# Keeping a weight fold's eight small products together on TensorE

## The chip, the cores and the metric

The kernel runs on one core of a Trainium2 chip. The metric is the device time of one launch in microseconds (us). The times of the kernel before are those of three runs; the trace comes from one more, profiled execution.

## What is computed

Nyström attention over 4 batches and 8 heads, followed by two feed-forward layers over all 2304 tokens, everything in float32 with double inputs for the weights:

```python
def _attn_ref(q, k, v):                      # (4, 8, 576, 64)
    q_lm, k_lm = ...                         # 32 landmarks: means over 18 rows
    A, Bm, C = sm(q, k_lm), sm(q_lm, k_lm), sm(q_lm, k)
    Z = Bm.T / (norm1 * norminf + 1e-06)
    for _ in range(6):
        Z = 2 * Z - Z @ Bm @ Z
    return A @ Z @ C @ v

x = attn_out.transpose(0, 2, 1, 3).reshape(B * S, H * D)
x = ((x @ w_a) * (x @ w_b)) @ w_out          # 512 -> 1536 -> 512
h = x @ w_in                                 # 512 -> 2048
g = h * np.tanh(softplus(h))
out = g @ w_out2                             # 2048 -> 512
```

## The kernel before

The attention output is never formed. For a batch b the small matrix M = Z C v (32 by 64 for each head) is multiplied into the first layer's weights: this is the **fold**. `MT[b]` holds M, two heads' halves on 64 partitions each; `wab[g]` holds columns of `w_a` and `w_b`, 256 of each, for group g (six groups of 512 columns). For one (b, g) the fold is eight products: 64 rows of `MT[b]` by 32 columns as the stationary operand, 64 rows by 512 columns of `wab[g]` as the moving one, each into its own 32 partitions of one of two PSUM banks (`ps_bm`, one pair buffer). ScalarE then copies the pair to `bm` (high part), and VectorE writes the remainder (low part). There are 4 x 6 = 24 folds. A product of float32 is two LDWEIGHTS and MATMUL records in the trace, so a fold has 16 records.

The layer itself follows in 96 slots, `ab(b, g, hf, ch)`: two halves of six 128x288 matmuls each (`ps_ab<-at,bm`), an evacuation by ScalarE (`ta`), a product by VectorE (`tg`), and a split of the result into `g1` by ScalarE and GpSimd. `emit_o1` sums `ps_o1<-g1,wo1`, six 128x288 matmuls for each half, and VectorE or ScalarE adds them to `x2acc`. The second layer (`ps_ab<-xc,wc` and the rest) begins at about 460 us and needs `x2acc` by way of DRAM (`x2d`, read as `xq`).

Weights arrive as float64 words in staging buffers (`stg`) through SyncE's DMA queue, and VectorE and ScalarE convert them (`wab`, `f`). A `wab` tile is filled in four pieces; columns j = 2 and 3 of its second axis come last. Each group is converted once, stored to DRAM and read back later through `load_wab`.

What sets the order on TensorE: the first part of the program is a list written by hand (`ORDER_1`), in which every instruction keeps the order of the text (`Written.on`). Four folds stand in it. After it `Written.on` is off, the slots are emitted in a loop, each calls `emit_bm` for the fold of a later slot, and a scheduler lays all instructions out by priority and by when it thinks that their inputs are there. A fold's eight products are independent for it, so it may put other matmuls between them. On each engine the chip then executes in the order that the scheduler wrote.

Of the kernel before, what the change touches and what calls it, by code (L numbers as in the profile page):

```python
# [31 lines left out]
def nystrom_moe_kernel(ctx: ExitStack, tc: tile.TileContext, q, k, v, w_a, w_b, w_out1, w_in2, w_out2, q1, k1, out):  # L32
# [30 lines left out]
    ac, pe, ve = Written(nc.scalar), Written(nc.tensor), Written(nc.vector)  # L63
# [18 lines left out]
    def pair_bank(tag):  # L82
        return two.get(tag, ps).tile([128, 2, 512], F32, tag=tag, bufs=1, name=f"ps_{tag}")
# [28 lines left out]
    MT = {}  # L112
# [382 lines left out]
    wab, converted = {}, {}  # L495
# [61 lines left out]

    def fold(b, g):
        p = pair_bank("bm")
        for c in range(2):  # L560
            r = slice(64 * c, 64 * c + 64)
            for j in range(4):
                pe.matmul(
                    p[32 * j:32 * j + 32, c], MT[b][r, 32 * j:32 * j + 32],
                    wab[g][r, j].rearrange("p a f -> p (a f)"), start=True, stop=True,
                )
        t = main.tile([128, 2, 2, 512], F32R, tag="bm", bufs=3, name="bm")
        yield
        ac.activation(t[:, 0], p, AF.Copy)
        yield  # L570
        ve.tensor_tensor(t[:, 1], p, t[:, 0].bitcast(F32), op=ALU.subtract)
        bm[b, g] = t

    def emit_bm(b, g):
        for _ in fold(b, g):
            pass
# [239 lines left out]
    for n in range(N_UNITS):  # L816
        part[f"c{n}"] = unit(n)
    part["f0"], part["f1"], part["F0"], part["F1"] = fold(0, 0), fold(0, 1), fold(1, 0), fold(1, 1)
    for n in range(N_SLOTS):
        b, m = divmod(n, 8)  # L820
        g, hf = (m // 2 % 2, m // 4) if b else (m // 4, m // 2 % 2)
# [97 lines left out]
    def product(k, n):  # L919
        p = bank("ab")  # L920
        w, x = wc[n], xs[n // 8, k]
        m = 0
        for j in range(2):
            for sl, sr in ((0, 0), (0, 1), (1, 0)):
                pe.matmul(p[:, 0:TB], w[:, sl, P_W[k], j], x[:, sr, j], start=(m == 0), stop=(m == 5))
                m += 1
        return p
# [39 lines left out]
    def early_product(k):  # L967
        Written.on = True
        p = product(k, 0)
        Written.on = False  # L970
        return p
# [10 lines left out]
    p = early_product(1)  # L982
# [5 lines left out]
    p = early_product(2)  # L988
# [89 lines left out]
    for n in range(24):  # L1078
# [7 lines left out]
        for gap, k in enumerate(ORDER):  # L1086
            if gap == 1 and n in (1, 2):
                last_stores.pop(0)[1]()
            if n == 0:
                p = None if k in ORDER[:3] else early_product(k)  # L1090
            else:
                p = product(k, n)
# [71 lines left out]
```

## Time and profile before

| | |
|---|---|
| median of three runs | 831.23 us (830.99 to 831.99) |
| the profiled execution's own time | 834.0 us |
| its span in the trace | 832.2 us |
| TensorE busy | 797.8 us, 96% of the span |
| VectorE, ScalarE, GpSimd busy | 541.7, 361.1 and 141.9 us |
| mean granted TensorE clock | 0.988 |

In the profile PE is TensorE's matmul side, PEld its weight loads, DVE VectorE, ACT ScalarE, POOL GpSimd, and SP SyncE. Nearly every instruction goes through one helper, so its line is L56; groups are told apart by tile: `ps_bm<-wab,mt` are the folds, `ps_o` stands for the banks of `emit_o1`. A row of the timeline gives start, duration, engine, line, operation, tiles, partitions by columns, and the number of instructions merged; in brackets is the idle time before it and what ended it. The ends of matmuls are modelled and overlap what follows, so the start of the next row is the better measure of what a row cost.

### The profile page before, as it was taken

How to read it: one execution, taken by the hardware profiler on the slowest of the kernel's cores; microseconds unless marked ns; L12 is line 12 of the kernel's file. 1: busy time of each engine (PE TensorE's matmuls, PEld its weight loads, DVE VectorE, ACT ScalarE, POOL GpSimd, SP SyncE). 2: the span in 40 equal slices, each digit the busy share in tenths (PEclk: the TensorE clock that was granted, in tenths of full speed). 3: DMA queues.
4: the chain of work that ended last, by engine and by line, in shares of the span. 5: the costliest groups of instructions: out<-in, count | busy, mean ns of one | idle time of the engine just before them, and what ended most of it. 6: DMA issues, size and time to landing. Idle time of an engine off the chain costs nothing.

```text
span 832.2 us, 14803 instructions
## 1 busy us (share of the span) xinstructions
PE 797.8 (96%) x5854; PEld 689.5 (83%) x5854; DVE 541.7 (65%) x1012; ACT 361.1 (43%) x824; POOL 141.9 (17%) x143
## 2 busy tenths in 40 slices
PE   5869999999999999999999999999999999999998
PEld 3356778997787887888889889988999999899997
DVE  7868887895498498886796765768433447433433
ACT  3645845444334344454353543554332335332332
POOL 1011212222141242222221344330000000000000
PEclk9889999999999999999999999999999999999999
DMA  9977466558527748868324887878645545555502
GB/s 353 293 280 257 149 233 219 194 179 285 184 68 250 290 143 300 283 209 292 108 93 133 324 335 276 303 280 344 215 179 237 217 185 232 215 192 224 191 0 76
DMA packets 48732, 183.44 MB, mean 220 GB/s; under 512 B 4260, under 2 KB 12452, under 8 KB 39320
## 3 DMA queue, kind: packets, MB, share of 16 engines
q1 hardware_dynamic: 39832, 169.40, 57.1%
q10 hardware_dynamic: 8832, 13.11, 4.3%
q8 instruction: 46, 0.75, 0.4%
q14 instruction: 22, 0.18, 0.1%
HBM read 129.02 MB, written 53.48 MB: 219 GB/s over the span
## 4 chain that ended last, share of the span: by engine, by line
PE 78%; DVE 8%; DMA 7%; ACT 3%; issue 3%; SPq 1%; ACTq 0%; POOL 0%; DVEq 0%
PE ps_ab L56 35%; PE ps_o L56 22%; PE ps_bm L56 12%; PE ps_at L56 10%; DMA tok<-in_k_dram 2%; DMA kt<-in_k_dram 2%; DVE f L56 2%; DMA vt<-in_v_dram 1%; DMA stg<-in_moe_w_a_dram 1%; DMA stg<-in_moe_w_out_dram 1%; ACT sa L56 1%; DVE wab L56 1%; DVE bm L56 1%; DVE tg L56 1%; DVE s L56 1%
## 5 line engine op out<-in xcount | busy, mean ns | idle before, releaser
L56 PE MATMUL ps_ab<-xc,wc 128*128 128x384 f32 x1008 | 197.1, 336 | 1.2 <-DVE u2s L56 1.0
L56 PE MATMUL ps_ab<-at,bm 128*128 128x288 f32 x1152 | 186.6, 302 | 4.7 <-DVE tg L56 3.5
L56 PEld LDWEIGHTS ps_ab<-xc,wc 128*128 128x128 f32 x1008 | 178.5, 188 | 12.5 <-DVE u2s L56 1.4
L56 PEld LDWEIGHTS ps_ab<-at,bm 128*128 128x128 f32 x1152 | 160.9, 189 | 30.2 <-issue 9.2
L56 PE MATMUL ps_o<-g,wo 128*128 128x288 f32 x1152 | 180.1, 299 | 3.7 <-ACT x2acc L56 3.0
L56 PEld LDWEIGHTS ps_o<-g,wo 128*128 128x128 f32 x1152 | 161.7, 190 | 18.4 <-issue 5.5
L608 POOL TENSOR_TENSOR g<-tg,g 128x288 fp32r<-128x288 f32 x96 | 88.7, 925 | 337.6 <-ACT g L56 274.2
L56 ACT ACTIVATE m<-c 128x384 f32<-128x384 f32 x95 | 49.6, 522 | 176.6 <-DVE c L56 174.5
L56 PE MATMUL ps_bm<-wo,g 128*128 128x512 f32 x288 | 92.8, 391 | 0.0
L56 DVE TENSOR_TENSOR g<-m,g 128x384 fp32r<-128x384 f32 x96 | 62.2, 650 | 30.5 <-ACT g L56 30.0
L56 PE MATMUL ps_at<-wo,g 128*128 128x512 f32 x288 | 81.5, 391 | 0.0
L56 PE MATMUL ps_o<-wo,g 128*128 128x512 f32 x288 | 78.7, 390 | 0.0
L56 DVE SCALAR_TENSOR_TENSOR f<-stg,f 128x512 uint32<-128x512 uint32 x88 | 69.8, 796 | 1.4
L56 ACT ACTIVATE g<-tg 128x288 fp32r<-128x288 f32 x96 | 42.4, 441 | 58.1 <-DVE tg L56 57.4
L56 ACT ACTIVATE ta<-ps_ab 128x288 f32<-128x288 f32 x96 | 38.9, 406 | 63.1 <-PE ps_ab L56 60.1
L56 PEld LDWEIGHTS ps_at<-wo,g 128*128 128x128 f32 x288 | 54.0, 188 | 10.2
L56 DVE TENSOR_TENSOR tg<-ps_ab,ta 128x288 f32<-128x288 f32 x96 | 43.3, 451 | 28.9 <-PE ps_ab L56 22.5
L56 PEld LDWEIGHTS ps_o<-wo,g 128*128 128x128 f32 x288 | 53.6, 188 | 8.7
L56 PEld LDWEIGHTS ps_bm<-wo,g 128*128 128x128 f32 x288 | 53.4, 188 | 6.3
L56 ACT ACTIVATE g<-m 128x384 fp32r<-128x384 f32 x96 | 50.4, 525 | 3.0
L56 DVE TENSOR_TENSOR u2s<-ps_ab,m 128x384 f32<-128x384 f32 x24 | 13.4, 557 | 57.9 <-PE ps_ab L56 57.9
L56 DVE TENSOR_TENSOR c<-ps_ab,m 128x384 f32<-128x384 f32 x23 | 12.8, 558 | 48.6 <-PE ps_ab L56 48.6
(156 smaller groups left out, 803.4 us busy)
## 6 DMA issues: line engine op xcount, KB each, us to landing
wc<-wcd SPq DMA_DIRECT2D x16, 1792.0 KB, 7.4
wo<-wod SPq DMA_DIRECT2D x16, 1024.0 KB, 9.5
stg<-in_moe_w_out_dram SPq DMA_DIRECT2D x28, 512.0 KB, 5.1
wcd<-wc SPq DMA_DIRECT2D x8, 1792.0 KB, 10.6
wab<-wabd SPq DMA_DIRECT2D x10, 1024.0 KB, 7.5
stg<-in_moe_w_in_dram SPq DMA_DIRECT2D x16, 512.0 KB, 6.0
wod<-wo SPq DMA_DIRECT2D x8, 1024.0 KB, 8.4
stg<-in_moe_w_a_dram SPq DMA_DIRECT2D x12, 512.0 KB, 7.4
```

What stands on the lines that cost most here:

```text
L56: i = f(*a, **kw)
L608: gp.tensor_tensor(t[:, 1], tg, t[:, 0].bitcast(F32), op=ALU.subtract)
```

## The change

The last piece of the weight tile is multiplied first, as an ordinary instruction; the other seven products are emitted at the scheduler's highest priority. So the one that must wait for the tile's last columns stands ahead, and behind it nothing else ready is preferred to the rest of the fold. The products, their operands and their number are the same.

```diff
     def fold(b, g):
         p = pair_bank("bm")
-        for c in range(2):
+        def piece(c, j):
             r = slice(64 * c, 64 * c + 64)
-            for j in range(4):
-                pe.matmul(
-                    p[32 * j:32 * j + 32, c], MT[b][r, 32 * j:32 * j + 32],
-                    wab[g][r, j].rearrange("p a f -> p (a f)"), start=True, stop=True,
-                )
+            pe.matmul(
+                p[32 * j:32 * j + 32, c], MT[b][r, 32 * j:32 * j + 32],
+                wab[g][r, j].rearrange("p a f -> p (a f)"), start=True, stop=True,
+            )
+
+        piece(0, 3)
+        with tc.high_priority():
+            for n in range(1, 8):
+                piece(n // 4, 3 - n % 4)
         t = main.tile([128, 2, 2, 512], F32R, tag="bm", bufs=3, name="bm")
```

What it does to the order: before, the 24 folds stand on TensorE in 39 places, 14 of them whole and 10 split in two to four; after it, in 24 places, all whole. Up to the first split fold the order on every engine is the same.

The first split fold, on TensorE, in the program's first third (x2 and x6 are the numbers of products, - is before, + is after):

```order
 L56 MATMUL ps_o_1298<-g_1191,wo_899 128x288 x3
-L56 MATMUL ps_bm<-wab,mt 32x512 x2
 L56 MATMUL ps_ab<-at,bm 128x288 x12
 L56 MATMUL ps_o_1349<-g_818,wo_620 128x288 x3
...
 L56 MATMUL ps_o_1349<-g_1191,wo_899 128x288 x3
-L56 MATMUL ps_bm<-wab,mt 32x512 x6
+L56 MATMUL ps_bm<-wab,mt 32x512 x8
 L56 MATMUL ps_ab<-at,bm 128x288 x6
```

The two products that stood ahead have joined the six; the matmuls between are where they were.

The first of the two folds that are split most, on TensorE, some 200 us into the program:

```order
 L56 MATMUL ps_o_2713<-g_2459,wo_2181 128x288 x3
 L56 MATMUL ps_o_2713<-g_2526,wo_2181 128x288 x3
-L56 MATMUL ps_bm<-wab,mt 32x512 x3
+L56 MATMUL ps_bm<-wab,mt 32x512 x8
 L56 MATMUL ps_at<-ident,E 128x128 x4
 L56 MATMUL ps_at<-ident,E 64x128
-L56 MATMUL ps_bm<-wab,mt 32x512
-L56 MATMUL ps_ab<-at,bm 128x288 x12
...
-L56 MATMUL ps_bm<-wab,mt 32x512
-L56 MATMUL ps_at<-rz 32x64 x8
-L56 MATMUL ps_ab<-at,bm 128x288 x12
-L56 MATMUL ps_bm<-wab,mt 32x512 x3
```

The fold's four places are now one, the first of them. From here on the scheduler lays out other matmuls anew too.

On SyncE's queue, where the second layer's first inputs (`xq`) are read among the loads of weights (`stg`), some 340 us into the program:

```order
 L416 DMA wab<-wabd_92 128x2048
 L441 DMA stg<-in_moe_w_in_dram 128x2x512
-L441 DMA stg<-in_moe_w_out_dram 128x1024
 L416 DMA xq<-x2d_83 128x2x384
 L416 DMA xq<-x2d_83 128x2x192
 L416 DMA xq<-x2d_84 128x2x192
-L441 DMA stg<-in_moe_w_out_dram 128x1024
+L441 DMA stg<-in_moe_w_in_dram 128x2x512
+L441 DMA stg<-in_moe_w_out_dram 128x1024 x2
```

The reads of `xq`, and the last reloads of `wab` with them, now stand ahead of two loads of weights that they stood behind, because the folds that free their buffers come earlier.

## Rows read from the trace of the kernel before

**Rows 1.** The page: busy time of each engine.
```profile
PE 797.8 (96%) x5854; PEld 689.5 (83%) x5854; DVE 541.7 (65%) x1012; ACT 361.1 (43%) x824; POOL 141.9 (17%) x143
```

**Rows 2.** Busy time by stretch of the span, all engines.
```profile
core 0: us, PE busy (x) PEld busy (x) DVE busy (x) ACT busy (x) POOL busy (x), PEclk, DMA share, GB/s
100.00:190.00 90.00, 87.64 (x738) 77.51 (x736) 75.46 (x145) 44.96 (x104) 21.23 (x24) 1.00 0.62 210
190.00:230.00 40.00, 40.00 (x403) 30.59 (x396) 20.18 (x47) 14.10 (x31) 7.96 (x9) 1.00 0.64 225
230.00:310.00 80.00, 78.96 (x871) 67.92 (x870) 62.03 (x132) 34.84 (x80) 23.65 (x26) 1.00 0.55 195
310.00:410.00 100.00, 99.14 (x733) 82.98 (x732) 78.65 (x137) 43.18 (x89) 25.09 (x26) 1.00 0.72 246
410.00:460.00 50.00, 47.66 (x334) 45.73 (x332) 39.82 (x70) 23.95 (x44) 11.19 (x12) 1.00 0.34 111
```

**Rows 3.** Whom TensorE waited for, 100 to 460: us, times, longest.
```profile
PE ps_ab L56 <- DVE tg L56: 3.1, 4, 1.0
PE ps_o L56 <- ACT x2acc L56: 1.2, 1, 1.2
PE ps_ab L56 <- ACT ta L56: 1.0, 2, 0.8
```

**Rows 4.** Timeline of TensorE around a split fold.
```profile
197.44 1.06 PE L56 MATMUL ps_bm<-wab,mt 64*32 64x512 f32 x6
198.43 0.76 PE L56 MATMUL ps_at<-ident,E 128*128 128x128 f32 x5
199.12 1.04 PE L56 MATMUL ps_bm<-wab,mt 64*32 64x512 f32 x2
200.10 1.86 PE L56 MATMUL ps_ab<-at,bm 128*128 128x288 f32 x12
201.79 1.75 PE L56 MATMUL ps_o<-g,wo 128*128 128x288 f32 x12
203.47 1.04 PE L56 MATMUL ps_bm<-wab,mt 64*32 64x512 f32 x2
204.45 0.43 PE L56 MATMUL ps_at<-rz 32*32 32x64 f32 x16
```

**Rows 5.** Timeline of TensorE where no small product is near.
```profile
141.66 1.76 PE L56 MATMUL ps_o<-g,wo 128*128 128x288 f32 x12
143.25 1.75 PE L56 MATMUL ps_ab<-at,bm 128*128 128x288 f32 x12
144.84 0.96 PE L56 MATMUL ps_o<-g,wo 128*128 128x288 f32 x6
```

**Rows 6.** Fold instructions alone: two stretches, then the whole group (busy, mean ns).
```profile
196.00:224.00 28.00, 7.36 (x32) 1.00 (x32) 0.00 (x0) 0.00 (x0) 1.00 0.61 208
263.00:274.00 11.00, 3.27 (x48) 0.54 (x48) 0.00 (x0) 0.00 (x0) 1.00 1.02 383
...
L56 PE MATMUL ps_bm<-wab,mt 64*32 64x512 f32 x384 | 42.0, 608 | 0.2 <-DVE bm L56 0.2
```

**Rows 7.** Chain that ended last, 95 to 131, and two rows of TensorE's timeline.
```profile
100.64 8.44 DMA stg<-in_moe_w_a_dram
117.20 8.28 DMA stg<-in_moe_w_out_dram
...
110.11 1.84 PE L56 MATMUL ps_o<-g,wo 128*128 128x288 f32 x12 [1.24 <-ACT x2acc L56]
129.17 1.86 PE L56 MATMUL ps_ab<-at,bm 128*128 128x288 f32 x12 [0.94 <-DVE tg L56]
```

**Rows 8.** Timeline of TensorE: two waits for a PSUM bank.
```profile
267.21 1.06 PE L56 MATMUL ps_ab<-at,bm 128*128 128x288 f32 x6 [0.25 <-ACT ta L56]
275.03 0.67 PE L56 MATMUL ps_ab<-at,bm 128*128 128x288 f32 x3 [0.78 <-ACT ta L56]
```

**Rows 9.** What SyncE's queue waited for, 150 to 420: us, times, longest.
```profile
SPq L441 <- DVE f L56: 139.7, 27, 21.6
```

## The prediction

> **What bounds the kernel now.** I began with the page: TensorE is busy for 797.8 us, 96% of the span [rows 1]. The table by stretches shows whether this holds where the folds are split: from 100 to 410 us TensorE is busy for 87.64 of 90, all of 40, 78.96 of 80 and 99.14 of 100 us, at a granted clock of 1.00 (the upper of its two levels, 2.4 GHz), while VectorE, the next busiest, has 75.46, 20.18, 62.03 and 78.65 [rows 2]. The list of waits says the same from the other side: from 100 to 460 us its longest entries are 3.1, 1.2 and 1.0 us [rows 3]. So a microsecond taken from TensorE's own work there should mostly come off the end.
>
> Next I read the timeline around a split fold, start to start [rows 4]. Six records of a fold begin at 197.44 and the next row at 198.43: 0.99 us. Two records begin at 199.12, the next row at 200.10: 0.98 us. Two more at 203.47: 0.98 us. A place costs nearly the same whether one product stands in it or all eight: alone, three whole folds take 3.27 us, 1.09 each, and the two folds that are split into seven places 7.36, or 1.05 for each place [rows 6]. The eight products write separate partitions and run side by side: sixteen records of 608 ns on average [rows 6] pass in 1.09 us. So a product that is sent ahead alone costs as much as the whole fold.
>
> **What the change removes.** On TensorE the folds stand in 39 places before (their 42.0 us busy in all are 1.08 each [rows 6]) and in 24 after: 15 fewer.
>
> - A removed place: 15 x 0.98 us = 14.7 us [rows 4].
> - Its edges. Twelve full-height matmuls behind a place take 1.69 us (200.10 to 201.79), twelve ahead of one 1.68 (201.79 to 203.47) [rows 4]; with no small product near, 1.59 (141.66 to 143.25, and again to 144.84) [rows 5]. That is 0.10 and 0.09 us for each place with full-height work on both sides. A place next to other small products, as at 203.47 and 204.45, saves less; I counted the unbroken stretches of small products in the order: 76 before, 63 after. 13 x 0.19 = 2.5 us.
>
> Sum: 17.2 us of TensorE's time.
>
> The rows leave the first weight load behind a fold uncovered. The Trainium skill's page "TensorE: Matmul & The Clock Gate" says in its opening table that the engine's queue pulls weight loads ahead of matmuls in flight; by that the edges would be nothing, the sum 14.7 us and my forecast 821.1. No such overlap is seen in 1.69 against 1.59 us, so the rows decide.
>
> **What is given back.**
>
> - The first two places removed lie before 129 us, and there TensorE isn't what ends last. The chain runs through loads of weights: 8.44 us from 100.64, 8.28 from 117.20; behind the first TensorE waited 1.24 us at 110.11, behind the second 0.94 at 129.17 [rows 7]. A TensorE that is 1.17 us earlier waits that much longer. I take all of it away: 2 x 1.17 = 2.3 us (bounds 0 and 2.3).
> - The new order has four runs of eighteen `ps_ab` matmuls, three halves in a row, where before there was one. There are two banks, so the third half needs the first one's evacuation. Such waits were 0.25 and 0.78 us [rows 8]: three more at these ends are 0.8 to 2.3 us, nothing if ScalarE is at hand. I take 0.8, since the list of waits has only 1.0 us for ScalarE's `ta` in all [rows 3].
> - From 410 to 460 us TensorE already idles for 50 - 47.66 = 2.3 us [rows 2], mostly behind VectorE's `tg`. The seven places removed between 310 and 410 us (7 x 1.17 = 8.2 us) bring it there earlier, VectorE's work staying the same. Bounds: 0, if VectorE's idle time moves along, since in 310 to 410 it has 21.35 us of it; 8.2, if it doesn't. VectorE has work for 118.5 of the 150 us from 310 to 460, and of 141.8 that is 84%: nearer the first, so I take 1.5.
> - The waiting of a fold for its last piece, now ahead of the other seven, costs nothing: the second part of a split fold stood behind the same piece before, and TensorE reaches it behind the same matmuls. All later folds read a tile that came back from DRAM as one.
>
> 17.2 - 2.3 - 0.8 - 1.5 = 12.6 us. The profiled execution took 834.0 us (span 832.2), 0.3% over the median of 831.2; a difference of 12.6 us carries over unchanged: 831.2 - 12.6 = **818.6 us**. Its own range is 814 (nothing given back) to 822 (the first two terms at their upper ends, the third at 3 us).
>
> **Rivals.**
>
> - *VectorE takes over from 310 us on.* Then the last seven places are worth nothing: 17.2 - 2.3 - 8.2 = 6.7 us, **824.5**. For it: it is busy for 78.65 of 100 and 39.82 of 50 us there [rows 2], it works its instructions off in the order written, and `tg` is what TensorE waits for most [rows 3]. Against: where the rest of its time is idle, TensorE isn't waiting. The Trainium skill's "TensorEngine Tiling (Array Packing)", section "PSUM Bottleneck", speaks for this one: packing speeds up TensorE and not the evacuation, which may become the limit.
> - *The waits of before shrink too.* The order is new from 190 us on, and the 5.3 us of waits in [rows 3] need not be there again: nothing given back and some 2 us more, **812**.
> - *The places are hidden anyway.* If TensorE had other waits to fill, as before 129 us, nothing is gained: **831**. Against: 6.6 us idle is all it has from 100 to 460 us, beside 17.2 to remove [rows 2].
> - *Slower: the loads of weights fall behind.* On SyncE's queue the reads of `xq` now stand ahead of two weight loads, and they wait for a buffer that a fold frees and for stored results. Each buffer goes round: VectorE frees it, SyncE loads it (8.3 us [rows 7]), VectorE converts it; the queue spent 139.7 us in 27 waits on that [rows 9]. A round late is 8.4 us on VectorE, then on `tg`, then on TensorE. It decides once TensorE loses more than 17.2 - 2.3 - 0.8 = 14.1 us; two rounds are 16.8, so 831.2 + 2.7 = **833.9**. For it: this loop is the chain from 100 to 129 us. Against: after that TensorE waits for `tg` four times, 1.0 us at most.
>
> That the products would not stay together is ruled out by the order itself.
>
> **How the numbers follow.** Forecast 0.62; VectorE takes over 0.17; waits shrink 0.10; hidden 0.05; slower 0.06. About 0.2% (1.7 us) is what a measurement can tell from no change. Faster: 0.62 + 0.17 + 0.10, and a little of the hidden case, 0.90; no change 0.04; slower 0.06. The range 814 to 825 holds nearly all of the forecast, most of the VectorE case and half of the shrinking waits: about 8 in 10.
>
> **What would show it.** The changed kernel's fold matmuls at about 24 x 1.09 = 26 us busy instead of 42.0; TensorE's total down by about 16; the wait for `x2acc` or weights near 110 and for `tg` near 129 us longer by about 1 us each; the second layer starting some 12 us earlier; `tg` waits between 400 and 440 us longer by 1 or 2 us. The forecast is wrong if those last waits grow by 5 us or more (VectorE), if loads of `stg` end long waits of ScalarE that TensorE inherits (slower), or if a lone place turns out to cover work that must then be done elsewhere.

## The result, and the profile after

The changed kernel takes 818.4 us (median; 817.2 to 820.7) against 831.3 us before: the ratio is 0.985 (95% interval 0.983 to 0.987). In a second set of runs, beside 831.75 us of the kernel before, it took 817.5 us, ratio 0.983 (0.981 to 0.984). The profiled execution took 818.37 us, its span 816.6 us.

The page of after, busy time of each engine, answers to [rows 1]:

```profile
PE 779.2 (95%) x5854; PEld 687.2 (84%) x5854; DVE 540.7 (66%) x1012; ACT 360.6 (44%) x824; POOL 140.2 (17%) x143
```

TensorE has 18.6 us less to do with the same 5854 matmuls (1.4 of it is a lower clock near 85 us in the profile of before, last section); the other engines have what they had, to within 2 us. The group of the folds (busy, mean ns of one, then the idle time ahead of them) shows where the time went, beside [rows 6]:

```profile
L56 PE MATMUL ps_bm<-wab,mt 64*32 64x512 f32 x384 | 26.3, 605 | 0.5 <-DVE bm L56 0.5
```

It had been 42.0 us for 39 places; it is 26.3 for 24, 1.10 each. Next the same stretches as in [rows 2], of after:

```profile
core 0: us, PE busy (x) PEld busy (x) DVE busy (x) ACT busy (x) POOL busy (x), PEclk, DMA share, GB/s
100.00:190.00 90.00, 86.25 (x741) 77.31 (x740) 76.78 (x151) 45.53 (x100) 20.72 (x24) 1.00 0.63 217
190.00:230.00 40.00, 40.00 (x470) 34.85 (x476) 24.68 (x54) 15.89 (x36) 10.04 (x11) 1.00 0.62 222
230.00:310.00 80.00, 78.81 (x851) 67.18 (x836) 59.69 (x125) 34.81 (x81) 23.87 (x26) 1.00 0.56 199
310.00:410.00 100.00, 97.77 (x780) 89.96 (x780) 83.76 (x149) 46.38 (x96) 23.76 (x28) 1.00 0.71 241
410.00:460.00 50.00, 48.67 (x304) 45.54 (x303) 39.09 (x64) 23.40 (x41) 13.54 (x10) 1.00 0.57 200
```

From 190 to 230 us TensorE is as full as before, but makes 470 instructions instead of 403: the places' time is filled with other matmuls. The first stretch idles more, 3.75 us against 2.36. VectorE is busier from 310 to 410 (83.76 against 78.65), and TensorE idles there 2.23 instead of 0.86 us, yet from 410 to 460 it idles 1.33 instead of 2.34.

Fixed windows compare different work, so I also read when ScalarE copies a fold to `bm`: the 4th, 8th, 13th and last fold. ScalarE's timeline of before:

```profile
94.33 1.00 ACT L56 ACTIVATE bm<-ps_bm 128x1024 fp32r<-128x1024 f32 x1
146.64 1.03 ACT L56 ACTIVATE bm<-ps_bm 128x1024 fp32r<-128x1024 f32 x1 [0.49 <-PE ps_ab L56]
259.80 1.03 ACT L56 ACTIVATE bm<-ps_bm 128x1024 fp32r<-128x1024 f32 x1 [1.78 <-PE ps_bm L56]
411.82 1.01 ACT L56 ACTIVATE bm<-ps_bm 128x1024 fp32r<-128x1024 f32 x1
```

and of after:

```profile
93.51 1.00 ACT L56 ACTIVATE bm<-ps_bm 128x1024 fp32r<-128x1024 f32 x1
145.56 1.03 ACT L56 ACTIVATE bm<-ps_bm 128x1024 fp32r<-128x1024 f32 x1 [0.49 <-PE ps_ab L56]
253.16 1.03 ACT L56 ACTIVATE bm<-ps_bm 128x1024 fp32r<-128x1024 f32 x1 [1.67 <-PE ps_bm L56]
395.72 1.03 ACT L56 ACTIVATE bm<-ps_bm 128x1024 fp32r<-128x1024 f32 x1 [0.33 <-PE ps_ab L56]
```

I start at the 4th fold, since the program up to it is the same and its time varies from one execution to the next by up to 4 us. From 4th to 8th fold (two places removed) after is 0.26 us shorter, from 8th to 13th (six removed) 5.56, from 13th to last (seven removed) 9.46; from the last fold to the end it is 0.50 longer. In all 14.8 us. The second layer runs at its old pace: its first matmul (`ps_ab<-xc,wc`) stands at 431.24 us instead of 446.86 (not at about 460, as I had it), and from there to the end both kernels take 385.3 us.

What TensorE waited for between 100 and 460 us (total, times, longest), beside [rows 3]:

```profile
PE ps_ab L56 <- ACT ta L56: 3.3, 6, 1.4
PE ps_ab L56 <- DVE tg L56: 1.8, 3, 0.9
PE ps_o L56 <- ACT x2acc L56: 1.8, 1, 1.8
PE ps_o L56 <- POOL g L612: 0.6, 1, 0.6
PE ps_bm L56 <- DVE bm L56: 0.5, 1, 0.5
```

The waits for ScalarE's `ta` have grown from 1.0 to 3.3 us, that for `x2acc` from 1.2 to 1.8; those for VectorE's `tg` have shrunk from 3.1 to 1.8. TensorE's timeline around the first two folds that were split shows those before 129 us, beside [rows 7]:

```profile
101.60 1.09 PE L56 MATMUL ps_bm<-wab,mt 64*32 64x512 f32 x16
102.61 1.07 PE L56 MATMUL ps_ab<-at,bm 128*128 128x288 f32 x6
...
109.03 1.85 PE L56 MATMUL ps_o<-g,wo 128*128 128x288 f32 x12 [1.80 <-ACT x2acc L56]
110.72 1.49 PE L56 MATMUL ps_ab<-at,bm 128*128 128x288 f32 x10
112.04 2.68 PE L56 MATMUL ps_o<-g,wo 128*128 128x288 f32 x19
...
121.93 1.06 PE L56 MATMUL ps_ab<-at,bm 128*128 128x288 f32 x6 [0.54 <-ACT ta L56]
123.46 1.09 PE L56 MATMUL ps_bm<-wab,mt 64*32 64x512 f32 x16 [0.47 <-DVE bm L56]
...
128.08 1.87 PE L56 MATMUL ps_ab<-at,bm 128*128 128x288 f32 x12 [0.94 <-DVE tg L56]
```

The folds stand whole (x16 records), and what they save is waited away: 1.80 us for `x2acc` instead of 1.24, then 0.54 and 0.47 us that were not there or shorter, and the 0.94 for `tg` again.

Of the 3.3 us behind `ta`, 0.54 stand in these rows. Two others of TensorE's timeline, and ScalarE's rows ahead of the larger one:

```profile
323.96 1.06 PE L56 MATMUL ps_ab<-at,bm 128*128 128x288 f32 x6 [1.39 <-ACT ta L56]
406.37 1.87 PE L56 MATMUL ps_ab<-at,bm 128*128 128x288 f32 x12 [0.56 <-ACT ta L56]
```

```profile
322.04 0.66 ACT L451 ACTIVATE f<-stg 128x512 f32<-128x512 f32 x1 [2.27 <-DVE f L56]
322.60 1.01 ACT L56 ACTIVATE bm<-ps_bm 128x1024 fp32r<-128x1024 f32 x1
323.50 0.41 ACT L56 ACTIVATE ta<-ps_ab 128x288 f32<-128x288 f32 x1
```

Before the 1.39 us ScalarE wasn't busy: it stood idle for 2.27 us until, by the profile, VectorE was done with a weight tile `f`, and the copy of the fold and the `ta` that frees the bank stand behind that conversion in its order.

### The profile page after: what moved, and what is told of

Read it like the earlier page. It is cut to its first block, busy times and chain, and to the rows that moved or that the text cites. A ratio compares the mean times of both kernels' runs of the same rounds, so it can differ in the third digit from the quotient of the medians.

```text
span 816.6 us, 14799 instructions
## 1 busy us (share of the span) xinstructions
PE 779.2 (95%) x5854; PEld 687.2 (84%) x5854; DVE 540.7 (66%) x1012; ACT 360.6 (44%) x824; POOL 140.2 (17%) x143
## 4 chain that ended last, share of the span: by engine, by line
PE 79%; DVE 11%; DMA 4%; ACT 3%; issue 2%; SPq 0%; ACTq 0%; DVEq 0%
PE ps_ab L56 35%; PE ps_o L56 22%; PE ps_bm L56 11%; PE ps_at L56 10%; DMA kt<-in_k_dram 2%; DVE f L56 2%; DVE wab L56 1%; ACT sa L56 1%; DMA stg<-in_moe_w_a_dram 1%; DVE tg L56 1%; DVE s L56 1%; DMA stg<-in_moe_w_out_dram 1%; DVE xt L56 1%; DVE stB L56 0%; DVE kl L56 0%
## 5 line engine op out<-in xcount | busy, mean ns | idle before, releaser
L56 PEld LDWEIGHTS ps_ab<-xc,wc 128*128 128x128 f32 x1008 | 178.5, 188 | 12.9 <-DVE u2s L56 1.3
L56 PE MATMUL ps_o<-g,wo 128*128 128x288 f32 x1152 | 176.8, 297 | 4.1 <-ACT x2acc L56 3.5
L612 POOL TENSOR_TENSOR g<-tg,g 128x288 fp32r<-128x288 f32 x96 | 86.9, 905 | 324.2 <-ACT g L56 262.5
L56 DVE TENSOR_TENSOR u2s<-ps_ab,m 128x384 f32<-128x384 f32 x24 | 13.4, 557 | 57.6 <-PE ps_ab L56 52.0
```

The costliest lines, as they stand in the source:

```text
L56: i = f(*a, **kw)
L612: gp.tensor_tensor(t[:, 1], tg, t[:, 0].bitcast(F32), op=ALU.subtract)
```

## The experiments

The theory: a place of small products costs TensorE some 0.98 us plus its edges, however many products stand in it, and a removed one comes off the end unless TensorE was waiting there. The rivals: that the priority alone, or the new order of everything else, does it; that a place costs by its products; that one group of folds carries the gain. In each of the first six kernels only `fold` is edited.

**Which folds.** Four kernels use the change for some folds only; the list `folds`, empty at first, counts them. The condition below is that of first_two; in pair it is `len(folds) in (11, 12)`, in late `len(folds) > 12`, in not_first `len(folds) > 6`.

```diff
-        piece(0, 3)
-        with tc.high_priority():
-            for n in range(1, 8):
-                piece(n // 4, 3 - n % 4)
+        folds.append(None)
+        if len(folds) in (5, 6):
+            piece(0, 3)
+            with tc.high_priority():
+                for n in range(1, 8):
+                    piece(n // 4, 3 - n % 4)
+        else:
+            for n in range(8):
+                piece(n // 4, n % 4)
```

First the two split folds before 129 us:

> Only the first two split folds are kept together, the rest is emitted as before: 37 places on TensorE instead of 39. Theory (a removed place is worth 1.17 us of TensorE, but before 129 us loads of weights set the pace): 2.3 us less work, 2.3 us more waiting, 831.3, at most 0.5 us faster; in the trace the waits near 110 and 129 us are longer. Rival 1 (every place is worth its full price): 829.0. Rival 2 (the gain of the whole change comes from the order that the scheduler lays out anew later, not from the places): also 831.3, so this run tells only the theory from rival 1.

Measured: ratio 0.9997 (0.9985 to 1.0010), no change. Then the two folds near 200 us, seven places to two:

> Only the two folds that are split into seven places near 200 us are kept together: 34 places instead of 39, 73 unbroken stretches of small products instead of 76. Theory: 5 x 0.98 + 3 x 0.19 = 5.5 us, 825.8, with waits of at most 1 us given back. Rival 2 (the later order is what gains; here it is mostly that of before): 830 to 831. Rival 3 (VectorE or the weight loads set the pace here too): 831.

Ratio 0.993 (0.991 to 0.995), 831.75 to 826.9 us. Then the folds from the 13th on, 39 places to 32:

> Only the folds from the thirteenth on, after 250 us, are kept together: 32 places instead of 39, 69 stretches instead of 76. Theory: 7 x 1.17 = 8.2 us less 1.5 of waiting, 824.6. Rival 1 (no waits added): 823.1. Rival 3 (VectorE sets the pace from 310 us on): 831.

Ratio 0.993 (0.991 to 0.994), 826.5 us, 1.9 us short of what was expected. And all but the first two:

> All folds but the first two split ones are kept together: 26 places, 65 stretches. Theory: the whole gain of the change is here, 818.4 within 0.7. Rival 1 (every place worth its price): 818.4 + 2.3 = 820.7.

Ratio 0.982 (0.980 to 0.984), 817.2 us: not slower than the whole change. Run once more beside the change itself:

> The change as it is, beside the next run on the same chip: 818.4 us as before.

> The change for all but the first two split folds, for the difference to the run before: if those two places are worth nothing, 818.4, give or take 0.7; if they are worth their price, 820.7. The earlier reading, 817.2, would be confirmed if it is again faster by over 1 us than the whole change.

817.5 (ratio 0.983, 0.981 to 0.984) and 816.7 us (0.982, 0.980 to 0.983). The first two places are worth nothing; whether undoing them gains 0.8 us isn't resolved, the intervals overlap. No one group carries the gain: the pair brings what it is priced at (5.7 us for 5.5), the late places 6.0 us for 8.2, and 1.7 us of the 2.2 between them are new waits in the list.

**Which half of the edit.** Priority for all eight products in the old order, and the new order without priority:

```diff
-        piece(0, 3)
         with tc.high_priority():
-            for n in range(1, 8):
-                piece(n // 4, 3 - n % 4)
+            for n in range(8):
+                piece(n // 4, n % 4)
```

> All eight products at the highest priority, in the order of before (the last piece isn't first): 27 places, three folds still split in two, all three among those whose weights are being converted; 68 stretches. Theory: two of the three extra places cost nothing, the third 1.17, and of the five more stretches one edge each: 818.4 + 1.2 + 0.4 = 820.0. Rival 1: 818.4 + 3 x 1.17 = 821.9. Rival 2 (the later order is what gains): as the changed kernel, 818.4, or anywhere else without regard to the places.

```diff
-        piece(0, 3)
-        with tc.high_priority():
-            for n in range(1, 8):
-                piece(n // 4, 3 - n % 4)
+        for n in range(8):
+            piece(n // 4, 3 - n % 4)
```

> The last piece first, at ordinary priority: 30 places, 70 stretches; the first two split folds are whole, five later ones are split in two or three. Theory: against the changed kernel 6 x 0.98 + 7 x 0.19 = 7.2 us more of TensorE's work, less some waiting that this covers: 824.5 to 825.6. Rival 2: no relation to the places.

Priority alone: 824.3 us, ratio 0.991 (0.988 to 0.994), so 4 us short of what was expected. Order alone: 826.9, ratio 0.993 (0.990 to 0.996), 1.3 to 2.4 us short. Neither half does what both do: they leave three and six more places. Part of the shortfall is in their rows. With order alone a part is the clock near 110 us (below the table). With priority alone, the second layer has a wait that neither before nor after has, and late has the same one (1.47 us at 454.74):

```profile
447.20 0.40 PE L56 MATMUL ps_at<-wo,g 128*128 128x512 f32 x1
449.04 0.51 PE L56 MATMUL ps_bm<-wo,g 128*128 128x512 f32 x1 [1.45 <-DVE g L56]
```

**What a place costs.** The change, and ahead of each of 24 `ps_ab` halves one more small product into columns of the bank that nobody reads (left out of the output); in the second kernel four (`range(4)`), side by side on the four 32-partition strips:

```diff
+        if w == 0 and 26 <= at[0] < 50:
+            for t in range(1):
+                pe.matmul(p[32 * t:32 * t + 32, 288:416], ident[0:64, 32 * t:32 * t + 32],
+                          ident[0:64, :], start=True, stop=True)
```

> The changed kernel with work added that nothing needs: ahead of 24 halves of a slot (slots 26 to 49) one product of 64 rows by 32 columns with 128 columns moving, into columns of the same PSUM bank that nobody reads. 24 more places, 84 stretches instead of 63. Theory (a place costs what one product takes through the array, whoever stands in it, plus its edges): from the trace's 0.35 us for 64 columns and 0.65 for 288, some 0.43 us for 128: 24 x 0.43 + 21 x 0.19 = 14.3 us, 832.7. Rival 4 (a product costs its share of a full place, an eighth): 24 x 0.43 / 8 = 1.3, 819.7.

> As the run with one added product, but four at each of the 24 points, into four separate groups of 32 partitions: 96 products in 27 places, 77 stretches. Theory: 27 x 0.45 + 14 x 0.19 = 14.8 us, 833.2, the same as with a quarter of the products. Rival 4 (cost by the product): four times what the run with one product adds, 57 us if that one adds 14.3.

TensorE's timeline of the kernel with one:

```profile
158.13 0.40 PE L56 MATMUL ps_ab<-ident 64*32 64x128 f32 x2
158.46 1.06 PE L56 MATMUL ps_ab<-at,bm 128*128 128x288 f32 x6
```

and with four:

```profile
156.81 0.42 PE L56 MATMUL ps_ab<-ident 64*32 64x128 f32 x8
157.16 1.06 PE L56 MATMUL ps_ab<-at,bm 128*128 128x288 f32 x6
```

One product of 128 columns takes 0.33 us start to start, four take 0.35, and with 512 columns a place takes 0.98 [rows 4]: it is priced by its columns, not by its products. In time the 24 lone products cost the change some 15 us: 833.1 us, ratio to before 1.002 (1.000 to 1.004). The forecast of 832.7 is met, but by another sum: 24 x 0.33 = 7.9 us instead of 10.3, 21 more unbroken stretches of small products at 0.19, 4.0 us, and 2.6 us of longer waits, which it left out. Four times as many products came to 826.5 us, ratio 0.993 (0.991 to 0.996), less than the lone ones, where products that cost one by one would have cost four times as much. It is also 6.7 us less than was expected. Not the price makes it less: 27 places at 0.35 and 14 more stretches are 12.1 us, the lone ones 11.9. From the 4th fold to the end it has 8.5 us of listed waits where the lone ones have 12.6, so 4.1 of the 6.5 us between the two are waits; the rest is open.

The edge behind a place can be seen in the timeline of before, in two narrow windows behind the place that ends at 200.10 [rows 4]:

```profile
200.10 0.40 PE L56 MATMUL ps_ab<-at,bm 128*128 128x288 f32 x1
200.34 0.56 PE L56 MATMUL ps_ab<-at,bm 128*128 128x288 f32 x3
```

The second full-height matmul starts 0.24 us after the first; where no small product is near they follow each other by 1.59 / 12 = 0.13 us [rows 5].

**What holds TensorE before 129 us.** The loads of weights in the first part of the program move half of their bytes, and every conversion reads that half twice (the conversions' part of the edit isn't shown):

```diff
+        if Written.on and not spare:
+            t = t[:, 0:256]
+            if shape is not None:
+                v, src = v[:, 0:1], src[:, 0:1]
+            else:
+                v, src = v[:, 0:512], src[:, 0:512]
         nc.sync.dma_start(out=v, in_=src)
```

> The kernel before, but each load of weights into `stg` in the first part of the program moves half of its bytes (the other half of a tile repeats the first, so the weights are wrong); every conversion keeps its size. A base line for the next run. If the loads alone set the pace between 100 and 129 us, the two waits there (1.24 and 0.94 us) go and the time falls by some 2 us, to about 829; if VectorE's conversions set it, the waits stay and the time with them, 831.3.

> The same halved loads, and the change for the first two split folds alone. If these two places were worth nothing because TensorE waited for the loads there, they are now worth 2 x 1.17 = 2.3 us against the run with halved loads (829 to 826.7). If VectorE's conversions hold TensorE there, or a place in this stretch costs nothing in itself, the two runs are equal to within 0.7 us.

828.56 us (ratio to before 0.996, 0.994 to 0.998) and 828.58 us. Halving the loads gains 2 us or more, and the waits at 110 and 129 us are gone: between the 4th and the 8th fold TensorE waits for nothing that the list of waits names, and that stretch is 2.5 us shorter. The intervals reach 1.4 to 1.7 us to either side, so the equal times alone hardly rule out a difference of 2.3 us; the rows say more. The list for the first two folds whole, same stretch of program (90.47 to 139.49 us):

```profile
PE ps_ab L56 <- DVE tg L56: 1.0, 1, 1.0
PE ps_ab L56 <- DVE bm L56: 0.4, 1, 0.4
PE ps_ab L56 <- ACT ta L56: 0.3, 1, 0.3
PE ps_bm L56 <- DVE bm L56: 0.2, 1, 0.2
```

and its busy times from 95 to 131 us:

```profile
95.00:131.00 36.00, 34.80 (x286) 30.22 (x285) 32.87 (x60) 22.99 (x57) 8.16 (x9) 1.00 0.61 213
```

1.9 us of new waits stand against 2.3 us of places removed, and between the 4th and the 8th fold 0.75 us are left of the gain. Without the long loads the places are still worth little: 1.6 of the 1.9 us are waits for VectorE, which is busy for 32.87 of 36 us. So my expectation of 2.3 us fell, and the rows speak for the rival in it, VectorE.

**Places and waits together.** For each kernel: places removed at 0.98 us and stretches of small products removed at 0.19; the change in TensorE's listed waits from the 4th fold to the end, against 7.4 us before; what the two give; what its profiled execution gained over that of before from the 4th fold to the end; and what the ratio of the timed runs is worth at 831.5 us. For the two with added products, these are taken off the price at 0.33 or 0.35 us a place (the second number of places).

| kernel | places, stretches | priced | waits | sum | profile | timed (95%) |
|---|---|---|---|---|---|---|
| after | 24, 63 | 17.2 | +2.6 | 14.6 | 14.8 | 12.6 (11.0 to 14.3) |
| after, again | 24, 63 | 17.2 | +2.3 | 14.9 | 13.2 | 14.5 (13.1 to 15.8) |
| not_first | 26, 65 | 14.8 | +0.2 | 14.6 | 15.1 | 14.9 (13.4 to 16.4) |
| not_first, again | 26, 65 | 14.8 | +0.7 | 14.1 | 15.2 | 15.4 (14.2 to 16.6) |
| prio_only | 27, 68 | 13.3 | +2.6 | 10.7 | 9.5 | 7.3 (4.9 to 9.8) |
| order_only | 30, 70 | 10.0 | +1.2 | 8.8 | 5.1 | 5.8 (3.6 to 8.0) |
| late | 32, 69 | 8.2 | +1.7 | 6.5 | 7.2 | 6.0 (4.8 to 7.2) |
| pair | 34, 73 | 5.5 | -0.1 | 5.6 | 7.1 | 5.7 (4.2 to 7.2) |
| first_two | 37, 74 | 2.3 | +1.8 | 0.5 | 0.8 | 0.2 (-0.8 to 1.2) |
| four | 24 and 27, 77 | 5.1 | +1.1 | 4.0 | 5.0 | 5.5 (3.3 to 7.6) |
| lone | 24 and 24, 84 | 5.3 | +5.2 | 0.1 | -0.3 | -1.6 (-3.1 to 0.0) |

For nine of the eleven, places less waits is what the profile shows, to 1.5 us. The other two, order_only and the change's second profile, are 3.7 and 1.7 off, and both have the same thing in their rows: after the wait for `x2acc` near 110 us the granted clock fell. TensorE's timeline of the change's second profile, and the table by stretches there (columns as above):

```profile
108.10 2.47 PE L56 MATMUL ps_o<-g,wo 128*128 128x288 f32 x12 [2.07 <-ACT x2acc L56]
110.37 2.44 PE L56 MATMUL ps_ab<-at,bm 128*128 128x288 f32 x10
112.65 0.55 PE L56 MATMUL ps_o<-g,wo 128*128 128x288 f32 x3
```

```profile
107.50:112.50 5.00, 4.40 (x21) 4.40 (x22) 2.39 (x5) 2.36 (x6) 0.00 (x0) 0.66 0.35 107
```

The granted clock is 0.66 over these 5 us. The 22 matmuls take 4.55 us start to start, and 4.55 in order_only; in after's first profile 3.01 (109.03 to 112.04). The 1.54 us account for the second profile's difference, and leave some 2 us of order_only open. Why prio_only's timed runs gain 3 us less than its rows say is open too.

The timed runs bear the sum out less well: it lies above their interval for prio_only (by 0.9 us), order_only (0.8), the first set of after (0.3) and lone (0.1), and 0.1 below it for the second of not_first. No run lays the order out anew and keeps all 39 places; that the gain is the places, and not the new order, rests on this sum and on the two kernels with added places.

## Why the prediction was right, step by step

The forecast, 818.6 us, is met by 818.4 and 817.5. Its steps fared differently.

- **A removed place, 0.98 us, and its edges, 0.19.** Right. The folds' busy time went where it was expected (26.3 us for "about 26"), TensorE's total fell by 18.6 instead of 16, which is the priced 17.2 and 1.4 of clock, and the kernels with added products show that a place costs the same with four as with one. Between the 8th fold and the end, where 13 places went, the change gains 14.5 and 14.9 us by its two profiles; 14.8 were priced for them. Against three profiles with before's order there (first_two and the two with halved loads), which needed 0.3 to 1.0 us less than before's own, it is 13.5 to 14.5, although the listed waits there grew by 0.4 to 1.1 us. The places alone, 13 x 0.98, are 12.7, so at least a part of the edges is needed. One of the two edges is in the rows of before themselves, 0.24 against 0.13 us (above). The opening table of the Trainium skill's page "TensorE: Matmul & The Clock Gate", by which weight loads are pulled ahead and the edges would be nothing, would have given those 12.7; the runs are 0.8 us or more above it. The Trainium skill's "TensorEngine Tiling (Array Packing)", section "Key Properties", says that tiles work in parallel and that changing the mode drains the engine: the first agrees with 0.33 against 0.35 us; how much of a place is the drain, no run here tells.
- **The first two places give nothing, 2.3 us.** Right in size: first_two changes nothing, not_first is no slower than the whole. The cause was told too narrowly. The wait for `x2acc` grew by 0.56 us and that for `tg` near 129 us not at all, where 1 us each was expected; the rest went into waits for `ta` and `bm`. Loads do end the wait near 110 us, and halving them gains 2 us or more; but with them halved new waits, 1.6 us for VectorE's `tg` and `bm` and 0.3 for ScalarE's `ta`, take back 1.9 of the 2.3 us.
- **Waits for ScalarE's `ta`, 0.8 us.** Too small, and for a reason that didn't come. The four runs of eighteen `ps_ab` matmuls are there, at 157.72, 338.83, 404.76 and 421.93 us, but none of their third halves waits; only at the one from 404.76 TensorE waits for `ta` at all, 0.28 us ahead of the first half and 0.56 ahead of the second. The list grew by 2.3 us; that this is the upper end of the bounds is chance. Of the 3.3 us, 0.54 belong to the first two places, and 1.39 stand at 323.96, where the `ta` came late because ScalarE had waited for VectorE's `f`.
- **VectorE in the late stretch, 1.5 us.** Wrong. The seven places removed there brought 9.5 us in the profile, and the `tg` waits between 400 and 440 us, which were to grow by 1 or 2 us, fell from 1.66 to 0.18. 8.2 were priced; the profiled execution of before was itself slow there: three kernels with its order in that stretch needed 0.7 to 1.2 us less for it, and against those the seven places are worth 8.3 to 8.8. So VectorE didn't become the bound: it had the idle time that [rows 2] show. A part of what it costs came by another way, through ScalarE's order, as the rows of the 1.39 us at 323.96 show; no run takes this wait away. The Trainium skill's "TensorEngine Tiling (Array Packing)", section "PSUM Bottleneck", says that the evacuation may become the limit; here the waits for it (`ta`) grew by 2.3 us, and TensorE is still busy for 97.77 of the 100 us from 310.
- **Nothing for the fold's wait on its last piece.** Right: the list of waits has no `wab` in it.
- **The difference of the profiled executions carries over unchanged.** It doesn't quite. Before's profile was 2.8 us over its median: 0.7 to 1.2 of that are the late stretch, and another 1.4 may be the clock near 85 us (below). The profiles differ by 15.6 us, the medians by 12.9 and 14.3.

Of the rivals, "the waits of before shrink too" came true for `tg` alone, and the two that needed the bound to move, to VectorE or to the loads on SyncE's queue, didn't come. That the number came out so close is in part luck: two of its deductions are off in opposite directions, 1.5 too small for ScalarE and 1.5 too large for VectorE. That places alone don't make a forecast is what prio_only shows: it was expected at 820.0 by its places and took 824.3.

## What to carry to other kernels

Small products that fill the array side by side should be counted in places, not in products: one sent ahead alone costs about as much as the whole set (0.98 against 1.09 us here), and a scheduler that takes them for independent may send it ahead, as it did with 10 of the 24 folds. What such a place is worth has to be read where it stands: by its columns, from the start of one row to the next, and at little or nothing if the engine waits a few rows later, as before 129 us. An order laid out anew brings waits of its own, here -0.1 to 5 us, which only its own run tells. The edit confined to the folds where the engine doesn't wait (not_first) lost nothing.

## What was not expected of the hardware

Waits of 2.07 and 2.05 us on TensorE, after a stretch at a granted clock of 1.00 (2.4 GHz), were followed by matmuls at the lower level (1.2 GHz) in two profiles (the change's second and order_only), at a cost of some 1.5 us each; waits of 2.08 us (first_two) and 2.18 us (four), at the same place in the program, were not. The same happened in the profile of before_half after 1.73 us, and in that of before:

```profile
85.58 4.98 PE L56 MATMUL ps_o<-g,wo 128*128 128x288 f32 x24 [1.76 <-ACT x2acc L56]
```

where after's, the same instructions behind nearly the same wait, ran on at the upper level:

```profile
84.75 3.62 PE L56 MATMUL ps_o<-g,wo 128*128 128x288 f32 x24 [1.74 <-ACT x2acc L56]
```

From the start of each row to the next one these are 4.82 and 3.46 us, a difference of 1.36 us. So a wait of this length can cost nearly as much again, in some executions and not in others, and the removed places before 129 us, which lengthen the wait near 110 us from 1.24 us to between 1.80 and 2.08, may buy a loss: that would fit not_first's 0.8 us, but isn't shown.
